# Sums of a 2x2 product scheme chained in PSUM, and scores issued behind a share of feed-forward

## The chip, the cores and the metric

The kernel runs on one core of a Trainium2 chip. The metric is the device time of one execution in microseconds (us). A core has five engines with instruction streams of their own: PE (TensorE, matrix products and transposes), ACT (ScalarE), DVE (VectorE), POOL (GpSimd) and SP (SyncE, which here only issues DMAs). They work in order, each on its own stream, and wait for each other by semaphores. Here PE writes to PSUM, ACT reads it from there, and POOL works in SBUF.

## The reference

Top-32 attention over 8 batches and 8 heads (576 positions, head size 64), then a feed-forward layer with ELU, all in fp32:

```python
scores = scale * np.matmul(q, k.transpose(0, 1, 3, 2))      # 8 x 8 x 576 x 576
kth = np.partition(scores, -32, axis=-1)[..., -32:-31]
scores = np.where(scores >= kth, scores, -1e9)
attn = np.exp(scores - scores.max(-1, keepdims=True))
attn = attn / (attn.sum(-1, keepdims=True) + 1e-9)
x = np.matmul(attn, v).transpose(0, 2, 1, 3).reshape(4608, 512)
h = x @ w_in                                                # 512 x 2048
g = np.where(h > 0, h, np.exp(np.minimum(h, 0)) - 1)
out = g @ w_out                                             # 2048 x 512
```

## The kernel before

**Attention in steps.** The work is cut into 144 steps, each one pair of heads times one tile of 128 queries. A step goes through a pipeline that is spread over four turns of the main loop. In turn `n`:

- PE computes the scores of step `n + 2` (`scores`, L335: eight matmuls of 64x128 tiles into two score tiles of PSUM, `wide[0]` and `wide[1]`, both called `scps` in the profile), and ACT evicts them to SBUF, scaled (L343, one instruction for each head);
- DVE selects the 32nd largest of each row of step `n` (`select`): per head, four MAX8 (L355, L369) with three MATCH_REPLACE8 (L362) between. The turn's four passes are these four rounds;
- ACT masks and exponentiates step `n - 1` (`mask`, L396 and L397), with a difference that POOL forms (`spread`, L376), and POOL normalises it (`normalise`, L407 to L414);
- PE transposes the probabilities of step `n - 2` (`turn`, L433) in three parts: four blocks (main), one block (rest) and four blocks (other); ACT copies them out (L434). The rest block has no PSUM tile of its own: it is written to the end of `wide[1]`;
- when the steps that go together are turned, `attend` (L459) multiplies them with the values, in 128x64 tiles, and ACT copies the result into `xT`, the input of the feed-forward layer (L486).

The k and q halves of later batches are loaded by SP (L235) into a few buffers, transposed by DVE (L289) and kept in `kqT`; v is loaded by SP (L269, L276). In the first turns DVE, ACT and POOL also decode the weights `w_in` and `w_out` (L179 to L196), in pieces that hang on DVE's passes.

**Feed-forward in shares.** The 4608 tokens make blocks: six of one tile of 128 tokens and fifteen of two. A block's pieces join the list `ffn` when its `xT` is complete. `feed(n, 0.25)` is called four times in a turn and takes pieces from the list by a budget, which is worked out from what is due when. A block has 16 `hidden` pieces (L534; ACT applies the ELU's parts, L544 to L553; the last addition is on POOL, L504, or in the early part on DVE, L506). A one-tile block then has four `project` pieces (L562). A two-tile block has seven `product` pieces.

**The 2x2 scheme.** A two-tile block multiplies its activations (two row halves, two column halves of 1024: a11, a12, a21, a22) with `w_out` (b11, b12, b21, b22) by seven products in place of eight. `product(j)` first forms a sum of quarters on POOL (L580, 128x1024, in `combine`), runs eight matmuls of 256 columns (L624, which the profile shows as 16 records) into a PSUM tile, and has ACT copy the result out (L629). Four of the seven weights are differences of quarters (`differences`, L681), kept in DRAM; `stream` (L663) loads them on SP, 256 KB a tile, four tiles a product, six tiles ahead: each tile that a product has used makes SP ask for another. The partial results are put together by POOL in SBUF (L580 again, 128x256, seven sums a block), and `emit` (L585) sends the rows out on SP.

The order in which instructions are issued on each engine is that of the program text: the scheduler is switched to manual. Everything depends on it, since each engine and each DMA queue takes its work in that order.

Of the kernel before, what the change touches and what calls it, by code (L numbers as in the profile page):

```python
# [9 lines left out]
ALU = mybir.AluOpType  # L10
FP32 = mybir.dt.float32
# [69 lines left out]
def kernel(  # L81
# [9 lines left out]
    nc = tc.nc  # L91
    P = nc.NUM_PARTITIONS
    B, H, S, D = q.shape
    dm, dff = moe_w_in.shape[0], moe_w_in.shape[1] // 2
# [7 lines left out]
    NG = NF // 2  # L102
# [11 lines left out]
    def pool(name, bufs, **kw):  # L114
        return ctx.enter_context(tc.tile_pool(name=name, bufs=bufs, **kw))
# [12 lines left out]
    ps_f = pool("ps_f", 2, space=PSUM)  # L128
# [77 lines left out]
    def settle():  # L206

        if decode or late or blocks[0].left or any(x[3] == 0 for x in ffn):
            return
        raws.close()  # L210
        late["f"] = ctx.enter_context(tc.tile_pool(name="f", bufs=2))
        late["g"] = ctx.enter_context(tc.tile_pool(name="g", bufs=2))
        late["x"] = ctx.enter_context(tc.tile_pool(name="xt", bufs=2))
        late["e"] = ctx.enter_context(tc.tile_pool(name="e", bufs=2))
        late["t"] = ctx.enter_context(tc.tile_pool(name="t", bufs=TB))
        late["in"] = ctx.enter_context(tc.tile_pool(name="in", bufs=2))
# [109 lines left out]
    def scores(u):  # L326

        u.sc = scpool.tile([P, 2, S], FP32, tag="sc", name="sc")
        q0 = (QUERIES if u.t.b == 0 else S) + u.t.qt * P
        for half in range(2):  # L330
            for h, i, rows in u.heads:
                kq = kqT[u.t.b, h // 2]
                part = slice(i * D, (i + 1) * D)
                k0 = (KEYS if i == 0 and u.t.b == 0 else 0) + half * HS
                nc.tensor.matmul(  # L335
                    wide[i][rows, half, 0:HS],
                    kq[part, q0 : q0 + u.t.ql],
                    kq[part, k0 : k0 + HS],
                    start=True,
                    stop=True,  # L340
                )
        for i in range(2):
            nc.scalar.activation(  # L343
                u.sc[:, i, :].rearrange("p (a s) -> p a s", a=2),
                wide[i][:, :, 0:HS], AF.Copy, scale=scale,
            )
# [147 lines left out]
    def close_gates(keep=0, upto=None):  # L494

        while gates:
            put, group, dst, n, apart = gates[0]
            if put > place[0] - keep if upto is None else group > upto:  # L500
                return
            gates.pop(0)
            if apart:
                nc.gpsimd.tensor_tensor(dst, n, dst, ALU.add)  # L504
                continue
            nc.vector.scalar_tensor_tensor(  # L506
                out=dst, in0=n, scalar=-1.0, in1=dst, op0=ALU.add, op1=ALU.add
            )

    def ffn_pieces(blk):  # L510
# [65 lines left out]
        def quarter(s, h):  # L576
            return blk.gT[h][:, :, s * P : (s + 1) * P]

        def combine(dst, x, y, op):
            nc.gpsimd.tensor_tensor(dst, x, y, op)  # L580

        def emit(s):
            for t in blk.tiles[s]:
                p0 = t.cols.start - s * P
                nc.sync.dma_start(out[t.rows, :], blk.o[s][p0 : p0 + t.ql, :])  # L585

        def product(j):
            left, right = slice(0, W), slice(W, dm)
            while blk.after:
                blk.after.pop(0)()  # L590
            if j == 7:
                return
            if j == 0:
                close_gates(upto=(blk.number, NF - 1))
                blk.o = [opool.tile([P, dm], FP32, tag="osb", name="osb") for _ in range(2)]
                blk.e = [late["e"].tile([P, W], FP32, tag="e", name="e") for _ in range(2)]
            a11, a12 = quarter(0, 0), quarter(0, 1)
            a21, a22 = quarter(1, 0), quarter(1, 1)
            c11, c12 = blk.o[0][:, left], blk.o[0][:, right]
            c21, c22 = blk.o[1][:, left], blk.o[1][:, right]  # L600
            e0, e1 = blk.e[0][:], blk.e[1][:]
            x, name, dst, after = (
                (a11, "b11", c11, [(a21, a21, a22, ALU.add)]),
                (a12, "b21", c12, [(a11, a21, a11, ALU.subtract)]),
                (a21, "t1", c22, [(a12, a12, a11, ALU.subtract)]),
                (a22, "t4", e0, [(a21, a22, a11, ALU.subtract)]),
                (a11, "t2", c21, [(c21, c21, c11, ALU.add), (c11, c11, c12, ALU.add)]),
                (a12, "b22", c12, [(c12, c12, c21, ALU.add), (c12, c12, c22, ALU.add)]),
                (a21, "t3", e1, [
                    (c21, c21, e1, ALU.add), (c22, c22, c21, ALU.add),  # L610
                    (c21, c21, e0, ALU.add),
                ]),
            )[j]
            if j == 0:
                combine(*after.pop())
            sums = ps_f.tile([P, dm], FP32, tag="f", name="ops")[:, left]
            for f in range(NG):
                if name[0] == "b":
                    w = w_out[:, NG * (name[1] == "2") + f, right if name[2] == "2" else left]
                else:  # L620
                    if f % TF == 0:
                        t = streamed.pop(0)
                    w = t[:, f % TF, :]
                nc.tensor.matmul(sums, x[:, f, :], w, start=f == 0, stop=f == NG - 1)  # L624
                if name[0] == "t" and f % TF == TF - 1:
                    stream()
            if 0 < j < 4:
                combine(*after.pop())
            nc.scalar.copy(dst, sums)  # L629
            blk.after += [lambda x=x: combine(*x) for x in after]  # L630
            if j > 4:
                blk.after.append(lambda: emit(j - 5))

        part = HIDDEN[blk.slots]
        behind = 2 * NF if blk.number else 0
# [14 lines left out]
        ]  # L650

    streamed, ahead_of = [], [0]
    names = ("t1", "t4", "t2", "t3")

    def stream():

        k = ahead_of[0]
        ahead_of[0] += 1
        if k >= 4 * QT * sum(x.slots == 2 for x in blocks):
            return  # L660
        t = late["t"].tile([P, TF, W], FP32, tag="t", name="tw")
        src = kept[names[k // QT % 4], k % QT]
        nc.sync.dma_start(t[:], src[:].rearrange("p (f n) -> p f n", f=TF))  # L663
        streamed.append(t)
# [35 lines left out]
    while ends:  # L700
        n = 1 if len(blocks) <= J else 2
        blk = Block(len(blocks), len(ends[:n]))
# [4 lines left out]
    for b in range(B):  # L707
# [15 lines left out]
        for qts in orders[b]:  # L723
# [3 lines left out]
            for qt in qts:  # L727
                n = len(steps)
# [12 lines left out]
    for b in range(1, B):  # L741
        f = first[b]
# [17 lines left out]
    def feed(n, share):  # L760

        place[0] += 1
        close_gates(2 if n > tight + 3 else 6)
        fed["at"] = max(fed["at"], n)
        ahead = [(w - fed["sum"]) / (x - fed["at"]) for x, w in due if x > fed["at"]]
        if ahead:
            fed["over"] += max(0.0, share * min(ahead))
        fed["at"] += share
        while ffn and decoded[0] >= ffn[0][1] and 0.5 * ffn[0][0] <= fed["over"]:
            cost, _, piece, _ = ffn.pop(0)  # L770
            fed["over"] -= cost
            fed["sum"] += cost
            piece()
            settle()
# [22 lines left out]
    def step(n):  # L797
        return steps[n] if 0 <= n < NS else None
# [3 lines left out]
    for n in range(NS + 3):  # L802
        for fn, args in todo.pop(n, []):
            fn(*args)
        ahead, cur, prev, done = step(n + 2), step(n), step(n - 1), step(n - 2)
        passes = select(cur, n < tight) if cur else iter(range(4))
        if ahead and n > 1:
            scores(ahead)
        if prev and n > tight:
            spread(prev)  # L810
        next(passes)
        feed(n, 0.25)
        while closing:
            attend(closing.pop(0))
        if prev:
            mask(prev, 0, n <= tight)
        if n > 1:
            turn_qk()
        next(passes)
        feed(n, 0.25)  # L820
        if done:
            turn(done, main)
            turn(done, rest)
        if prev:
            mask(prev, 1, n <= tight)
        next(passes)
        feed(n, 0.25)
        if done:
            turn(done, other)
        next(passes)  # L830
        if prev:
            normalise(prev)
        feed(n, 0.25)
        turn_qk(True)
        if n < 2:
            scores(ahead)
# [36 lines left out]
```

## Time and profile before

| quantity | value |
|---|---|
| three runs | 1600.43, 1596.32, 1598.8 us (median 1598.8) |
| profiled execution | 1596.33 us, of which the span on the core is 1594.5 us |
| mean granted clock of PE | 0.983 |
| PE busy | 1525.4 us (96%) |
| DVE busy | 1450.7 us (91%) |
| ACT busy | 1196.4 us (75%) |
| POOL busy | 938.5 us (59%) |
| 128x1024 sums on POOL (L580) | 60 of 2.37 us |
| 128x256 sums on POOL (L580) | 75 + 30 of 0.73 us |
| copies of products on ACT (L629) | 75 + 30 of 0.37 us |

Busy shares are means over the whole span. PE's idle time lies nearly all in the first 416 us, where the weights are decoded and DVE's selection sets the pace; behind that both PE and DVE are close to always busy. PE's records are pipelined, so the end of one lies beyond the start of the next; the distance from start to start is what a record costs.

In the lines of waits that follow, the name behind the arrow is the instruction whose end released the waiting one; the figures are the time waited in all, the number of waits and the longest, or, in a group's line, the busy time and the mean. In the lines of the timeline the first two numbers are start and duration, `x` tells how many instructions are put together, and the bracket is the idle time before them with its releaser. A stretch's line gives its bounds and its length, the busy time of PE, weight loads, DVE, ACT and POOL with the number of instructions, the granted clock, the DMA share and GB/s.

### The profile page before, as it was taken

The page shows a single profiled execution, that of the slowest core. Times are in us where ns is not written, and L with a number is a line of the kernel's source. Part 1 is how long each engine was busy: PE and PEld are TensorE (multiplying, and loading weights), DVE is VectorE, ACT ScalarE, POOL GpSimd, SP SyncE. Part 2 cuts the span into 40 slices and gives each one's busy share as a digit, 9 for nine tenths or more (in the row PEclk, how much of TensorE's full clock was granted, in tenths as well). Part 3 has the DMA queues.
Part 4 walks back from the last instruction along what each step waited for, and adds up shares of the span by engine and source line. Part 5 has one row for each costly group of instructions (what it writes and reads, how often), then busy time and mean ns, then how long its engine had stood idle before and what let it go on. Part 6 is the DMA issues. An engine that isn't in the chain of part 4 may idle for free.

```text
span 1594.5 us, 28265 instructions
## 1 busy us (share of the span) xinstructions
PE 1525.4 (96%) x9492; PEld 1180.7 (74%) x9492; DVE 1450.7 (91%) x2976; ACT 1196.4 (75%) x2460; POOL 938.5 (59%) x1596
## 2 busy tenths in 40 slices
PE   4789989999899999999999999999999999999999
PEld 2476667667677778877787778877777777887886
DVE  6899999999999799999999789999999969999800
ACT  6897666779586868696878777777768786869652
POOL 4984546446556565656566656565655656666651
PEclk9889989999999999999999999999999999999999
DMA  8622233012402243214421343214240414030320
GB/s 243 196 80 38 61 75 115 7 23 43 122 31 89 62 102 78 80 41 110 93 83 45 83 97 84 67 49 100 42 139 1 134 17 133 9 119 1 119 62 25
DMA packets 224912, 123.47 MB, mean 77 GB/s; under 512 B 182272, under 2 KB 183296, under 8 KB 224768
## 3 DMA queue, kind: packets, MB, share of 16 engines
q1 hardware_dynamic: 223568, 121.38, 28.0%
q8 instruction: 75, 1.23, 0.3%
q14 instruction: 69, 0.57, 0.1%
q10 hardware_dynamic: 1200, 0.30, 0.1%
HBM read 108.00 MB, written 13.63 MB: 76 GB/s over the span
## 4 chain that ended last, share of the span: by engine, by line
PE 68%; DVE 17%; ACT 8%; issue 3%; POOL 3%; DMA 1%; SPq 0%; DVEq 0%; ACTq 0%; POOLq 0%
PE hps L534 24%; PE ops L624 22%; PE avps L459 8%; PE scps L335 8%; DVE wk L362 7%; PE eps L433 6%; DVE m L369 5%; DVE m L355 2%; ACT sc L397 1%; ACT sc L396 1%; POOL tw L681 1%; ACT et L434 1%; DVE raw L192 1%; ACT n L553 1%; ACT n L544 1%
## 5 line engine op out<-in xcount | busy, mean ns | idle before, releaser
L369 DVE MAX8 m<-wk 128x8 f32<-128x576 f32 x864 | 609.0, 746 | 0.7 <-POOL den L376 0.7
L534 PE MATMUL hps<-xT,w_in 128*128 128x256 f32 (+1 forms) x2688 | 560.0, 356 | 0.0
L534 PEld LDWEIGHTS hps<-xT,w_in 128*128 128x128 f32 x2688 | 441.8, 192 | 77.1 <-issue 34.9
L362 DVE MATCH_REPLACE8 wk<-m,wk 128x576 f32<-128x576 f32 x576 | 423.1, 742 | 0.0
L397 ACT ACTIVATE sc<-sc,den 128x576 f32<-128x576 f32 x288 | 223.5, 776 | 61.2 <-POOL den L376 46.5
L407 POOL TENSOR_SCALAR dene<-den 128x2 f32<-128x2 f32 x144 | 32.5, 226 | 398.4 <-ACT sc L397 395.7
L624 PE MATMUL ops<-tw,gT 128*128 128x256 f32 x960 | 224.1, 386 | 10.5 <-DMA tw<-kept 10.4
L396 ACT ACTIVATE sc<-sc,m 128x576 f32<-128x576 f32 x288 | 225.1, 782 | 8.2 <-DVE m L369 8.2
L335 PE MATMUL scps<-kqT 64*128 64x288 f32 (+1 forms) x1280 | 200.6, 446 | 32.0 <-ACT et L434 18.2
L414 POOL TENSOR_SCALAR sc<-sc,rec 128x576 f32<-128x576 f32 x288 | 214.4, 755 | 14.9
L504 POOL TENSOR_TENSOR gT<-n,gT 128x512 f32<-128x512 f32 x136 | 173.6, 1277 | 75.5 <-ACT n L553 75.4
L355 DVE MAX8 m<-sc 128x8 f32<-128x576 f32 x288 | 201.9, 742 | 15.2 <-ACT sc L343 11.8
L624 PEld LDWEIGHTS ops<-tw,gT 128*128 128x128 f32 x960 | 178.4, 191 | 47.5 <-DMA tw<-kept 12.0
L362 DVE MATCH_REPLACE8 wk<-m,sc 128x576 f32<-128x576 f32 x288 | 211.5, 742 | 0.0
L343 ACT ACTIVATE sc<-scps 128x576 f32<-128x576 f32 x288 | 171.4, 649 | 48.9 <-PE scps L335 48.9
L459 PE MATMUL avps<-et,vT 128*64 128x256 f32 (+2 forms) x2320 | 194.1, 310 | 9.5 <-ACT et L434 9.4
L459 PEld LDWEIGHTS avps<-et,vT 128*64 128x64 f32 x2320 | 130.2, 141 | 76.2 <-issue 33.6
L335 PEld LDWEIGHTS scps<-kqT 64*128 64x128 f32 (+1 forms) x1280 | 106.9, 183 | 98.1 <-issue 36.9
L433 PE MATMUL eps<-ident,sc 128*128 128x128 f32 x1152 | 174.6, 277 | 1.2 <-ACT xT L486 0.8
L434 ACT COPY et<-eps 128x512 f32<-128x512 f32 x288 | 164.6, 572 | 9.6 <-PE eps L433 7.3
L433 PEld LDWEIGHTS eps<-ident,sc 128*128 128x128 f32 x1152 | 142.0, 143 | 32.8 <-issue 9.6
L624 PE MATMUL ops<-w_out,gT 128*128 128x256 f32 x720 | 164.4, 381 | 0.1
(56 smaller groups left out, 1570.1 us busy)
## 6 DMA issues: line engine op xcount, KB each, us to landing
tw<-kept SPq DMA_DIRECT2D x240, 256.0 KB, 3.2
raw<-in_moe_w_in_dram SPq DMA_DIRECT2D x16, 512.0 KB, 4.9
vT<-in_v_dram SPq DMA_DIRECT2D x64, 128.0 KB, 2.6
raw<-in_moe_w_out_dram SPq DMA_DIRECT2D x16, 512.0 KB, 4.2
out_dram<-osb SPq DMA_DIRECT2D x32, 256.0 KB, 2.4
kin<-in_k_dram SPq DMA_DIRECT2D x112, 72.0 KB, 2.4
qin<-in_q_dram SPq DMA_DIRECT2D x112, 72.0 KB, 2.5
kept<-tw SPq DMA_DIRECT2D x16, 256.0 KB, 2.0
```

Of the source, the lines that this page charges most:

```text
L335: nc.tensor.matmul(wide[i][rows, half, 0:HS], kq[part, q0 : q0 + u.t.ql], kq[part, k0 : k0 + HS], start=True, stop=True,)
L355: nc.vector.max(found[i], cur[i])
L362: nc.vector.match_replace(wk[i], found[i], cur[i], TAKEN)
L369: nc.vector.max(found[i], cur[i])
L396: nc.scalar.activation(sc, sc, AF.Prelu, scale=-1.0, bias=low, alpha=1.0 / STEEP)
L397: nc.scalar.activation(sc, sc, AF.Exp, scale=-STEEP, bias=gap, accum_out=u.den[:, i : i + 1])
L414: nc.gpsimd.tensor_scalar(u.sc[:, i, :], u.sc[:, i, :], rec[:, i : i + 1], 1.0, ALU.mult, ALU.mult)
L433: nc.tensor.transpose(ps[:, c * P : (c + 1) * P], sc[:, c0 : c0 + P], ident[:])
L434: nc.scalar.copy(g.et[:, chunks, u.at, :], ps[:, 0 : n * P].rearrange("p (c q) -> p c q", c=n),)
L459: nc.tensor.matmul(ps[i * D : (i + 1) * D, cols], vt[:, 2 * J + i if c == J else i * J + c, :], w, start=(c == 0), stop=(c == J),)
L534: nc.tensor.matmul(blk.h[:, f % bank, :], w_in[:, i, f * P : (f + 1) * P], blk.xT[:, i, 0:n_tok], start=(i == 0), stop=(i == NC - 1),)
L624: nc.tensor.matmul(sums, x[:, f, :], w, start=f == 0, stop=f == NG - 1)
```

## The change

There are two parts.

First, a block holds two PSUM tiles for all of its seven products, and three of their halves collect sums: `one` takes b11, then t2, then t3 on top of each other, `three` takes t1 and then b22, and `two` takes b21 and, opened anew, t4. ACT copies a half out after each product, the running sum included. The order of the products changes from b11, b21, t1, t4, t2, b22, t3 to b11, b21, t1, t2, b22, t3, t4, and with it the order in which the weights are streamed. POOL's sums of results go from seven to four a block; the four sums of quarters stay, in another order, and the a21 - a22 - a11 one is read by the last product. The first tile's rows are sent out one product earlier.

Second, from turn 2 on `scores(n + 2)` is issued behind the first share of feed-forward of its turn, directly ahead of `attend`, in place of the turn's start. On PE and on ACT (whose evictions are issued with it) the share and its activations now come first.

```diff
+                blk.s = [ps_f.tile([P, dm], FP32, tag="f", name="ops") for _ in range(2)]
...
-            x, name, dst, after = (
-                (a11, "b11", c11, [(a21, a21, a22, ALU.add)]),
-                (a12, "b21", c12, [(a11, a21, a11, ALU.subtract)]),
-                (a21, "t1", c22, [(a12, a12, a11, ALU.subtract)]),
-                (a22, "t4", e0, [(a21, a22, a11, ALU.subtract)]),
-                (a11, "t2", c21, [(c21, c21, c11, ALU.add), (c11, c11, c12, ALU.add)]),
-                (a12, "b22", c12, [(c12, c12, c21, ALU.add), (c12, c12, c22, ALU.add)]),
-                (a21, "t3", e1, [
-                    (c21, c21, e1, ALU.add), (c22, c22, c21, ALU.add),
-                    (c21, c21, e0, ALU.add),
+            one, two, three = blk.s[0][:, left], blk.s[1][:, left], blk.s[1][:, right]
+            x, name, sums, opens, dst, after = (
+                (a11, "b11", one, True, c11, [(a21, a21, a22, ALU.add)]),
+                (a12, "b21", two, True, e0, [(a11, a21, a11, ALU.subtract)]),
+                (a21, "t1", three, True, c22, [
+                    (a12, a12, a11, ALU.subtract), (c11, c11, e0, ALU.add),
                 ]),
+                (a11, "t2", one, False, c12, [(a21, a22, a11, ALU.subtract)]),
+                (a12, "b22", three, False, e1, [(c12, c12, e1, ALU.add)]),
+                (a21, "t3", one, False, c21, [(c22, c22, c21, ALU.add)]),
+                (a22, "t4", two, True, e0, [(c21, c21, e0, ALU.add)]),
             )[j]
             if j == 0:
-                combine(*after.pop())
-            sums = ps_f.tile([P, dm], FP32, tag="f", name="ops")[:, left]
+                combine(*after.pop(0))
...
-                nc.tensor.matmul(sums, x[:, f, :], w, start=f == 0, stop=f == NG - 1)
+                nc.tensor.matmul(
+                    sums, x[:, f, :], w, start=opens and f == 0, stop=f == NG - 1,
+                    skip_group_check=not opens,
+                )
...
             if 0 < j < 4:
-                combine(*after.pop())
+                combine(*after.pop(0))
             nc.scalar.copy(dst, sums)
             blk.after += [lambda x=x: combine(*x) for x in after]
-            if j > 4:
-                blk.after.append(lambda: emit(j - 5))
+            if j in (4, 6):
+                blk.after.append(lambda: emit(j // 2 - 2))
...
-    names = ("t1", "t4", "t2", "t3")
+    names = ("t1", "t2", "t3", "t4")
...
         passes = select(cur, n < tight) if cur else iter(range(4))
-        if ahead and n > 1:
-            scores(ahead)
         if prev and n > tight:
             spread(prev)
         next(passes)
         feed(n, 0.25)
+        if ahead and n > 1:
+            scores(ahead)
         while closing:
             attend(closing.pop(0))
```

## The prediction

> **What bounds the kernel now.** I read the engine totals first, then the busy time by stage, then PE's waits, then the order of records around the edit.
>
> ```profile
> PE 1525.4 (96%) x9492; PEld 1180.7 (74%) x9492; DVE 1450.7 (91%) x2976; ACT 1196.4 (75%) x2460; POOL 938.5 (59%) x1596
> ```
> ```profile
> 280.00:416.00 136.00, 130.38 (x744) 91.88 (x743) 134.79 (x279) 106.08 (x215) 69.14 (x131) 0.99 0.14 28
> 416.00:800.00 384.00, 380.68 (x2348) 300.26 (x2348) 372.79 (x767) 298.24 (x615) 229.15 (x404) 1.00 0.31 81
> 800.00:1200.00 400.00, 395.17 (x2458) 313.48 (x2456) 386.32 (x796) 310.91 (x641) 245.47 (x421) 1.00 0.29 79
> 1200.00:1520.00 320.00, 318.03 (x1986) 252.85 (x1986) 294.21 (x608) 248.34 (x515) 197.39 (x333) 1.00 0.23 67
> ```
>
> The second view is busy time by stretch: length, then PE, weight loads, DVE, ACT, POOL, clock, DMA. To 416 us DVE has no idle time and PE waits. Behind it PE does (1094 of 1104 us), so only what changes PE's stream there counts. POOL has 40% to spare: the 45 sums it loses (30 x 0.73 us of 128x256 with `osb` alone and 15 with `e`, 33 us in all) are worth nothing by themselves.
>
> ```profile
> PE scps L335 <- ACT et L434: 18.2, 9, 3.3
> PE ops L624 <- DMA tw<-kept: 10.4, 3, 5.6
> PE avps L459 <- ACT et L434: 9.4, 14, 1.0
> ```
>
> These are PE's waits: us, times, longest. The first lies before 280 us, where PE has slack. The second is three stalls, at 410 (5.62), 744 (1.38) and 1155 us (3.44), each in a streamed product whose weights were asked for late.
>
> **The change, part by part.**
>
> *Fewer shape switches on PE.* Scores are 64x128 tiles, value products 128x64, all else 128x128. Record to record a 256-column matmul takes 215 ns; the first of another shape takes 309 and the one behind it 105 ns too much, so a switch costs 0.2 us. With the scores directly ahead of the value products the built program has 391 switches for 445. Of the 54, 17 come before the stall at 410 us and are swallowed by it; 10 lie between 410 and 744 us (-2.0 us), 16 to 1155 (-3.2), 11 behind (-2.2). Bounds: 0.1 to 0.25 us each.
>
> *The rest transpose meets the eviction.* The rest transpose (L433, one 128x128) writes the unused end of a score bank, so it waits until ACT has evicted these scores (L343).
>
> ```profile
> 518.49 0.27 ACT L434 COPY et<-scps 128x128 f32<-128x128 f32 x1
> 520.28 0.59 ACT L434 COPY et<-eps 128x512 f32<-128x512 f32 x1
> 521.45 1.19 ACT L343 ACTIVATE sc<-scps 128x576 f32<-128x576 f32 x2 [0.58 <-PE scps L335]
> ```
>
> Here ACT stood ready and the two evictions ended 1.29 us behind the last score record (520.17 + 1.17, to 522.64). Before, a feed share (a product or hidden piece) lay between scores and transposes, so nothing waited. In the new order 11 steps behind 410 us run scores, four main transposes (0.44 us), rest transpose: no value product comes due in them and the share now stands ahead. The gap is 1.29 - 0.44 = 0.85 us: 3 steps to 744 us (+2.6), 3 to 1155 (+2.6), 5 behind (+4.3). In 17 more, one hidden piece lies between, 2.27 us; there ACT may first have to finish activations of the share ahead (four of 0.59 to 0.63 us, ending some 2.2 to 2.45 us behind), so 0 to 0.3 us, taken as 0.15 (+0.9, +0.9, +0.8). Where a value product is between (1.8 to 2.3 us and more) it covers. What queues behind the waiting transpose is all of PE, since matmuls run in order. Bounds 0 and 1.2 us a step.
>
> *The stream of weights.* It is asked for on SP in order, a tile for each tile used, six ahead. The last two tiles of a block (3 and 4 of the last product) are asked for by the last streamed product but one. That was followed by one more streamed product and one resident one; now the final product comes straight behind it, and the resident `b22` is past. So the request is one product (3.55 us) later against its use, and falls behind k and q loads (L235) that wait for a DVE transpose (L289) in two blocks. In block 8 (all four rows are of the kernel before):
>
> ```profile
> 1080.30 3.62 PE L624 MATMUL ops<-w_out,gT 128*128 128x256 f32 x16
> 1087.33 3.72 PE L624 MATMUL ops<-tw,gT 128*128 128x256 f32 x16
> ```
> ```profile
> 1089.54 0.76 DVE L289 STREAM_TRANSPOSE kqT<-kin 128x576 f32<-128x576 f32 x1
> ```
> ```profile
> 1090.32 0.33 SPq L235 DMA_DIRECT2D kin<-in_k_dram  x1
> ```
>
> At 1080.30 stands the last product but one (after: `t3`), at 1087.33 the last (after: `t4`), whose third tile begins 1.8 us in, at 1089.1. SP is held to 1090.3, issues two k loads (0.96) and then the tile; tiles land 3.2 us behind their issue (the page's median for `tw`). 1094.5 - 1089.1 = 5.4 us of stall. A stall of 5.62 us at 410 was followed by a half clock (8 records in 3.77 us for 1.89, +1.9 us), one of 3.44 by none; I add 1.9: +7.3 in all. In block 4 the same reckoning (transpose 759.33, last product 760.55): landing 764.5, wanted 762.3, +2.3 us and no half clock. In the other blocks no such load stands ahead, or the transpose it needs is long done. Bounds: 0 (tiles just in time) to 4 in block 4, 0 to 9 in block 8. The Trainium skill, "TensorE: Matmul & The Clock Gate", What's actually happening, has PE drop to half rate after one idle window of about 3.4 us that runs free of the kernel; by it a stall of 5.4 us may miss a whole window, and the sum would be 1.9 us lower; the trace's two long stalls, one with and one without, fit.
>
> *The old stalls.* At 410: with scores behind the first share ACT does two weight-decoding steps earlier near 46 us, where DVE waited 3.92 us for it, and one k load less stands ahead of the stream: PE resumes 1.8 us earlier (between 0 and 4). At 744: the landing follows DVE, which waits for the scores at 550 us ("DVE kqT L289 <- PE scps L335", three times, 37.8 us), now 1.7 us later; no gain. At 1155: DVE last followed PE at 921 us, so the landing moves with PE as of then (+2 to 3), while PE will be 7 or more later still by block 8: the 3.44 us are gone (-3.4).
>
> *The chains.* Sums are read three to five products in as before, with one POOL sum of 0.73 us ahead of `c22`'s operand; slack was 1.4 us and more save in one block: +0 to 1. The second and third product share a PSUM tile, so the third waits for ACT's copy (0.37 us, some 0.36 behind the product); in 4 of 15 blocks only 0.44 us of transposes stand between: 4 x 0.3 = 1.2 at most. Together +1, between 0 and 3; at nothing only if ACT is idle just then. The Trainium skill, "PSUM — Partial Sum Buffer", Summary: rules for kernel authors, wants PSUM guarded by bank when one engine reads what another fills; by that rule these waits can't be had away while the two halves share a bank. No run here shows it otherwise.
>
> **The sum**, against the profiled execution (1596.3 us, span 1594.5; the median of the three runs, 1598.8, is 2.5 higher):
>
> - to 744 us: -1.8 - 2.0 + 2.6 + 0.9 = -0.3; the kept wait at 744 puts it at about +0.8;
> - to 1155 us: block 4 +2.3, -3.2 + 2.6 + 0.9 = +0.3, block 8 +7.3, the old stall -3.4: +6.5;
> - behind: -2.2 + 4.3 + 0.8 = +2.9; chains +1.
>
> Together +11.2 us: 1607.5 for the execution; against the median 1610. Since block 8's price is the most uncertain I shade it by two and say 1608.
>
> **The rivals.**
>
> *Faster: the switches alone.* If ACT gets to the evictions in time or the tile framework lets the rest transpose go, the 28 waits are nothing, and if SP isn't held (DVE running some 5 us further ahead of PE than before, the point from which it decides), the stream is in time. Then -1.8 - 7.4 + 1 = -8 us, 1590. For it: DVE had waits for PE of up to 13.7 us, so it is ahead in places. Against: the rows in block 8 place the transpose behind the product already, with nothing in the change that hastens DVE there. Chance 0.24.
>
> *The evictions bite, the stream does not.* 0.8 + 0.3 + 2.9 + 1, that is +5: 1604. For it: stalls on the stream were three in 1596 us, and DMA latency varies. Chance 0.18.
>
> *Both bite*, as forecast: 1601 to 1616. Chance 0.5.
>
> *Worse:* the 17 short covers fail by a full 0.85 us (+12) or the half clock follows in block 4 too: 1617 to 1625. For it: ACT is 75% busy, and the evictions stand behind its activations now. Chance 0.08.
>
> *It does not do what it says* is no rival for the switches and the sums: both counts are in the built program.
>
> **How the numbers follow.** About 0.3% (4.8 us) is what a measurement of this kernel can tell from no change: 1594.0 to 1603.6. Faster takes the first rival's 0.24 less 0.02 for its slower end; same takes that 0.02, half of the second rival's chance less a little (0.08) and 0.06 of the forecast's low end: 0.16. The rest, 0.62, is slower. The range runs from 1591, which takes in the upper part of the first rival, to 1617, where only the worse case is beyond. The forecast's own range is 1601 to 1616.
>
> **What would show it.** Right: a new PE wait "scps L433 <- ACT sc L343" of 10 us or so in 11 to 28 places; a stall on `tw` near 1090 us of 3 us or more, one near 762, none near 1155; POOL busy 33 us less; gaps ahead of L335 and L459 fewer. Wrong: no wait at the rest transposes, or `tw` waits that sum to no more than 10.4 us, in which case it is the first rival.

## The result, and the profile after

The changed kernel takes 1605.4 us (median of six runs, 1604.2 to 1609.4) against 1598.5 of the kernel before: 1.0048 times as long, 95% interval 1.0031 to 1.0064, so 5 to 10 us slower. The forecast was 1608 us with 0.62 for slower. The profiled execution has a span of 1603.8 us, 9.3 more than before.

Two things in the description above have to be corrected. The manual order holds for PE, ACT, DVE and POOL alone; SP's order is laid out by the scheduler, which matters below. And the sum of quarters that is formed last (a22 - a11 in the code's names) is read by t3, not by the last product.

The totals by engine, then busy time by stretch (bounds, length, PE, weight loads, DVE, ACT, POOL, clock, DMA share, GB/s), of the changed kernel:

```profile
PE 1523.6 (95%) x9492; PEld 1182.3 (74%) x9492; DVE 1452.6 (91%) x2976; ACT 1200.0 (75%) x2460; POOL 903.3 (56%) x1551
```
```profile
416.00:800.00 384.00, 376.24 (x2331) 297.19 (x2329) 372.47 (x768) 298.33 (x614) 216.86 (x388) 1.00 0.30 79
800.00:1200.00 400.00, 391.18 (x2430) 310.52 (x2429) 383.20 (x788) 307.49 (x631) 232.20 (x403) 0.99 0.30 79
1200.00:1520.00 320.00, 313.74 (x1954) 248.78 (x1954) 294.80 (x608) 245.62 (x507) 185.41 (x318) 1.00 0.23 67
```

POOL is 35 us less busy and nothing came of it (its 45 sums fewer are 60 fewer with `osb` alone and 15 more with `e`). PE is busy for 1.8 us less in all, yet the kernel is longer: PE waits more behind 416 us, 22.8 us of 1104 instead of 10.1. PE's waits, in us, times and the longest:

```profile
PE scps L433 <- ACT sc L343: 12.2, 17, 0.8
PE ops L624 <- DMA tw<-kept: 11.9, 5, 5.0
PE scps L335 <- ACT et L434: 11.4, 6, 2.6
PE avps L459 <- ACT et L434: 9.8, 16, 1.9
```

The first row did not exist before: the rest transpose that waits for the eviction of the scores. One of the 17, in the timeline of PE and then of ACT (start, duration):

```profile
1146.13 1.24 PE L335 MATMUL scps<-kqT 64*128 64x288 f32 x8
1147.30 0.66 PE L433 MATMUL eps<-ident,sc 128*128 128x128 f32 x4
1148.73 0.30 PE L433 MATMUL scps<-ident,sc 128*128 128x128 f32 x1 [0.78 <-ACT sc L343]
```
```profile
1147.40 1.19 ACT L343 ACTIVATE sc<-scps 128x576 f32<-128x576 f32 x2 [0.79 <-PE scps L335]
```

ACT stood ready, started at once and ended at 1148.59; PE had only four transposes in between. From start to start PE loses 0.94 us here, as in ten other steps behind 410 us. Of the six others five lie earlier; the last, at 1386 us, is shorter (0.51 us), with a short value product in between.

The second row has a sum 1.5 us above that of before (10.4) and other places. The new long stall is in block 8 (PE, then SP):

```profile
1087.03 1.99 PE L624 MATMUL ops<-tw,gT 128*128 128x256 f32 x8
1094.06 3.78 PE L624 MATMUL ops<-tw,gT 128*128 128x256 f32 x8 [5.04 <-DMA tw<-kept]
```
```profile
1090.25 0.87 SPq L235 DMA_DIRECT2D kin<-in_k_dram  x2
1091.22 1.39 SPq L666 DMA_DIRECT2D tw<-kept  x3
```

The first half of the last product is through at 1089, the tiles of the second half are asked for at 1091.22, behind two k loads that waited for DVE. Behind the stall eight records take 3.78 us for 1.99: half the clock. The next is in block 4:

```profile
760.77 3.27 PE L624 MATMUL ops<-tw,gT 128*128 128x256 f32 x8 [2.39 <-DMA tw<-kept]
```

A third is short, and its cause another: SP was held not by a k load but by the first tile's output rows, which waited for a sum on POOL until 590.92 (PE, then SP). The same hold returns at the end of the experiments.

```profile
594.66 1.13 PE L624 MATMUL ops<-tw,gT 128*128 128x256 f32 x4 [0.96 <-DMA tw<-kept]
```
```profile
590.95 0.36 SPq L585 DMA_DIRECT2D out_dram<-osb  x1
591.40 1.36 SPq L666 DMA_DIRECT2D tw<-kept  x3
```

The steps' rest transposes, set against those of the kernel before, give the course: 1.3 us earlier at 408 us, 5.8 at 424, 3.5 at 742, 0.1 later at 764, 0.3 earlier at 1080, 7.2 later at 1091, 8.2 at 1152, 4.4 at 1165 and 9.2 at the end. So the loss has four main places: the two long new stalls (4.3 and 7.5 us with their half clocks), and two slopes of 2.2 us (424 to 742, of which the short new stall is 1.2) and 4.8 us (behind 1165); 1.0 us more comes between 1091 and 1152. Two old stalls gave back 4.5 and 3.7 us, the one at 744 another 0.6.

### The profile page after: what moved, and what is told of

The parts are those of the page before. It is cut to its first block, busy times and chain, and to the rows that moved or that the text cites. A ratio compares the mean times of both kernels' runs of the same rounds, so it can differ in the third digit from the quotient of the medians.

```text
span 1603.8 us, 28233 instructions
## 1 busy us (share of the span) xinstructions
PE 1523.6 (95%) x9492; PEld 1182.3 (74%) x9492; DVE 1452.6 (91%) x2976; ACT 1200.0 (75%) x2460; POOL 903.3 (56%) x1551
## 4 chain that ended last, share of the span: by engine, by line
PE 67%; DVE 13%; ACT 11%; POOL 5%; issue 3%; DMA 1%; SPq 0%; DVEq 0%; ACTq 0%; POOLq 0%
PE hps L534 24%; PE ops L624 18%; PE avps L459 8%; PE scps L335 7%; DVE wk L362 6%; PE eps L433 5%; DVE m L369 4%; PE ops L562 2%; ACT sc L397 2%; ACT sc L343 2%; DVE m L355 2%; ACT sc L396 1%; POOL tw L684 1%; ACT et L434 1%; POOL sc L414 1%
## 5 line engine op out<-in xcount | busy, mean ns | idle before, releaser
L534 PE MATMUL hps<-xT,w_in 128*128 128x256 f32 (+1 forms) x2688 | 550.8, 354 | 3.5 <-ACT gT L547 3.5
L624 PE MATMUL ops<-tw,gT 128*128 128x256 f32 x960 | 224.5, 387 | 12.8 <-DMA tw<-kept 11.9
L335 PE MATMUL scps<-kqT 64*128 64x288 f32 (+1 forms) x1280 | 196.6, 447 | 25.5 <-ACT kqT L311 13.4
L624 PEld LDWEIGHTS ops<-tw,gT 128*128 128x128 f32 x960 | 178.9, 192 | 46.0 <-DMA tw<-kept 14.5
L624 PE MATMUL ops<-w_out,gT 128*128 128x256 f32 x720 | 164.3, 381 | 0.1
```

The lines of the kernel that those rows point to most:

```text
L335: nc.tensor.matmul(wide[i][rows, half, 0:HS], kq[part, q0 : q0 + u.t.ql], kq[part, k0 : k0 + HS], start=True, stop=True,)
L534: nc.tensor.matmul(blk.h[:, f % bank, :], w_in[:, i, f * P : (f + 1) * P], blk.xT[:, i, 0:n_tok], start=(i == 0), stop=(i == NC - 1),)
L624: nc.tensor.matmul(sums, x[:, f, :], w, start=opens and f == 0, stop=f == NG - 1, skip_group_check=not opens,)
```

## The experiments

My theory was that of the prediction: a gain by fewer shape switches, a loss by the evictions and one by weights that are asked for too late. All times are medians; the kernel before, run beside them, had 1598.4 to 1598.8.

**One part at a time.** First the scores moved alone:

```diff
-        if ahead and n > 1:
-            scores(ahead)
...
         feed(n, 0.25)
+        if ahead and n > 1:
+            scores(ahead)
```

> The scores moved, the products as before. My theory (the loss is rest transposes that wait for the score evictions, plus a weight stream that asks too late; the switches are a gain): rest transposes wait about 0.94 us in 11 steps behind 410 us (+10.3), 37 fewer switches there at 0.2 us (-7.4), the start some 4 to 6 us earlier, and the stalls on the weights at 744 and 1155 us stay, none new near 758 and 1089. Sum -3 to +2 us on the kernel before: 1596 to 1600 us, clearly under the changed kernel's 1605.4. Rival one (later scores starve DVE's selection, so that the moved scores are the whole loss): 1603 to 1606, with DVE waiting for L343 in many steps. Rival two (the chained sums are the whole loss, the move is a pure gain): 1588 to 1592.

Measured: 1598.0 us, ratio 1.000 (0.9991 to 1.0008). The rest transposes wait 12.1 us in 17 places, as in the changed kernel; no stall at 758 or 1089, and those at 740 (2.0 us from start to start) and 1151 (3.1) stay. Neither rival holds: the move is neither the loss nor a gain. It starts 5.3 us early at 424 us and loses 4.9 to the end.

Then the chained sums and the new order of products alone:

```diff
         passes = select(cur, n < tight) if cur else iter(range(4))
+        if ahead and n > 1:
+            scores(ahead)
...
         feed(n, 0.25)
-        if ahead and n > 1:
-            scores(ahead)
```

(against the changed kernel, whose other lines it keeps)

> The sums chained in PSUM and the product order new, the scores where they were. My theory: no wait at the rest transposes and 445 shape switches as before, but the new stalls on the weights: about 2.4 us near 758 us with a half clock behind it (+1.4) and 5 us near 1089 us with a half clock (+2), while the 3.4 us at 1155 go; +1 for chains. Sum +6 to +9 us on the kernel before: 1604 to 1608. Rival one (the moved scores are the whole loss; 45 sums fewer on POOL help): 1595 to 1599. Rival two (sharing banks makes each product wait for the copy of the one before): 1609 or more, with PE waits for ACT's copies at L624.

Measured: 1603.7 us, ratio 1.0035 (1.0023 to 1.0048), just under the forecast's 1604. This part alone carries most of the loss, 5.2 of 7.0 us; the scores alone gained 0.4, so some 2 us belong to neither part by itself. PE's view of block 8:

```profile
1089.34 1.99 PE L624 MATMUL ops<-tw,gT 128*128 128x256 f32 x8
1096.64 1.65 PE L624 MATMUL ops<-tw,gT 128*128 128x256 f32 x3 [5.31 <-DMA tw<-kept]
```

The stall near 758 us is not there; the one at 744 is 0.4 us longer instead and has a half clock behind it. The step from 1080 to 1091 us is 7.7 us longer than before, and the stall at 1155 is gone (-3.7). No wait for a product's copy shows at L624, so the rival of the shared banks falls.

**The order of the products.** The changed kernel with t3 ahead of b22:

```diff
-                    (a12, a12, a11, ALU.subtract), (c11, c11, e0, ALU.add),
+                    (a21, a22, a11, ALU.subtract), (c11, c11, e0, ALU.add),
                 ]),
-                (a11, "t2", one, False, c12, [(a21, a22, a11, ALU.subtract)]),
-                (a12, "b22", three, False, e1, [(c12, c12, e1, ALU.add)]),
+                (a11, "t2", one, False, c12, [(a12, a12, a11, ALU.subtract)]),
                 (a21, "t3", one, False, c21, [(c22, c22, c21, ALU.add)]),
+                (a12, "b22", three, False, e1, [(c12, c12, e1, ALU.add)]),
...
-            if j in (4, 6):
-                blk.after.append(lambda: emit(j // 2 - 2))
+            if j > 4:
+                blk.after.append(lambda: emit(j - 5))
```

> The changed kernel with one edit: t3 is multiplied ahead of b22, so that the last two weight tiles of a block are asked for one product earlier against their use, as in the kernel before (the sum of quarters that t3 reads is formed one product earlier too). My theory: the stalls near 758 us (2.4 and 1.4 of half clock) and 1089 us (5 and 2) go, the one at 1155 us comes back (3.4 to 3.8): -7 to -8 us, 1597 to 1599. Rival (DMA latency, not the place in the queue, makes the stalls): they stay, 1604 to 1606. Risk: t3's sum of quarters has only one product of cover, so a POOL wait at L624 of up to 1 us a block (+0 to +15).

Measured: 1601.3 us, ratio 1.0020 (1.0011 to 1.0029): 4 us less, not 7 to 8. Both long new stalls are gone, the short one too, and that at 1155 is back (3.25 us), as expected, so the place in the queue makes them. Behind the stall at 1155 stands a half clock that the scores-only kernel has not (1.4 us). The rest went the way of the risk: from 1165 us to the end this kernel falls 5.7 us back where the scores-only one falls 3.0, with small waits of PE at the products, the longest for a sum of quarters on POOL (0.51 us) and for ACT's copy of a product (0.46).

**The wait at the rest transposes.** If this transpose is simply put later, its wait should go:

```diff
         if done:
             turn(done, main)
-            turn(done, rest)
...
         if done:
+            turn(done, rest)
             turn(done, other)
```

> The changed kernel with one edit: the rest transpose (into the end of a score bank) is issued behind the third share, ahead of the other transposes, instead of straight behind the main ones. My theory: 8 of the 11 waits of 0.94 us behind 410 us go (in 3 steps nothing lies between even now), so -7 to -8 us: 1597 to 1599, with 'scps L433 <- ACT sc L343' down from 12.2 us to 2 to 4. The stalls on the weights stay. Rival (the waits are only where PE's idle time shows and would turn up elsewhere, since ACT is the late one): 1603 to 1606, the wait moving to another line.

Measured: 1613.2 us, ratio 1.0095 (1.0077 to 1.0113). The expectation was wrong, and the rival right in its direction, though not in its size. The old wait fell to 2.3 us, as I had said, and another grew from 11.4 us:

```profile
PE scps L335 <- ACT et L434: 44.2, 23, 5.4
PE scps L433 <- ACT sc L343: 2.3, 3, 0.8
```

The shared bank binds in both directions: the next turn's scores overwrite the rest block, so they wait until ACT has copied it out, and ACT gets to that behind a mask and a share's activations (PE, then ACT):

```profile
1138.72 0.27 PE L433 MATMUL scps<-ident,sc 128*128 128x128 f32 x1
1143.08 1.23 PE L335 MATMUL scps<-kqT 64*128 64x288 f32 x6 [1.25 <-ACT et L434]
```
```profile
1142.78 0.25 ACT L434 COPY et<-scps 128x128 f32<-128x128 f32 x1
```

The other way to take the wait away is to move the scores only in turns in which value products are due; in the others the move saves no switch.

```diff
+        if ahead and n > 1 and not closing:
+            scores(ahead)
...
         feed(n, 0.25)
+        if ahead and n > 1 and closing:
+            scores(ahead)
         while closing:
```

It was applied to the kernel before, to the changed kernel, and to the one with t3 ahead of b22.

> The kernel before, with the scores moved only in turns in which value products are due; in the other turns they stay at the turn's start. The built program has the same 391 shape switches as the kernel with all scores moved, but a share of feed-forward lies between scores and rest transpose wherever no value product does. My theory: the 11 waits of 0.94 us of the scores-only run go and nothing else changes: 1598.0 - 10 = 1587 to 1589, 'scps L433 <- ACT sc L343' near 1 or 2 us. Rival (PE's time behind 410 us is set by DVE or ACT, so a wait taken away comes back as another): 1595 to 1599.

> The changed kernel with the same edit: scores moved only where value products are due. My theory: 1605.4 - 10 = 1594 to 1597, with the stalls on the weights near 758 and 1089 us left as they are. Rival as for the kernel with products as before: 1602 to 1606.

> Both edits on the changed kernel: t3 ahead of b22, scores moved only where value products are due. My theory: 1601.3 - 10 = 1590 to 1593, some 3 us above the one with the products as before, because the chained sums have less cover on POOL (three waits of 0.3 to 0.7 us for L580) and give nothing on PE. Rival (45 sums fewer on POOL are worth something once PE has no other waits): at or under the one with the products as before.

Measured: 1596.3 (ratio 0.9987, 0.9978 to 0.9996), 1600.2 (1.0009, 1.0000 to 1.0018) and 1599.1 us (1.0004, 0.9995 to 1.0013). All three are above what my theory gave, and the first lies where its rival had it. The waits at the rest transposes are all but gone, but only 2 to 5 us came of the 10. PE's waits in the first of the three tell where they went:

```profile
PE ops L624 <- DMA tw<-kept: 15.1, 3, 5.6
```

The three old stalls end when the weights land that SP asks for behind k loads, and these wait for DVE's transposes. The one ahead of the second stall, in the kernel before and in the first of the three:

```profile
738.73 0.75 DVE L289 STREAM_TRANSPOSE kqT<-kin 128x576 f32<-128x576 f32 x1
```
```profile
736.11 0.76 DVE L289 STREAM_TRANSPOSE kqT<-kin 128x576 f32<-128x576 f32 x1
```

The transposes come 4.0, 2.6 and 2.0 us earlier than in the kernel before and the stalls end 4.3, 2.6 and 1.1 us earlier, but PE is 4.2, 5.2 and 3.3 us ahead when it gets there. So the first stall keeps its length and PE waits longer in the others: 5.7, 4.2 and 5.7 us from start to start, with half clocks behind all three, for 5.8, 1.5 and 3.6 before, with one behind the first alone. On my theory the stalls had to stay as they were; I had treated them as fixed durations, where DVE sets their ends.

**The stalls themselves.** With a ring of seven tiles (`TF, TB = 2, 7`) on the first of these kernels:

> As the kernel before with scores moved where value products are due, and the ring of streamed weight tiles seven long for six. My theory of the stalls (a request held on SP behind k and q loads, a tile worth 0.89 us of products): each of the three stalls (about 3, 2 and 3 us) shrinks by 0.9 us, together with what half clock follows -2 to -4 us on the one with six: 1584 to 1586. Rival (the landing is set by DVE's transpose alone, and the held tile is the same one however long the ring): no change.

Measured: 1594.4 us, ratio 0.9968 (0.9955 to 0.9980): 1.9 us less than with six, just short of the 2 to 4 that were forecast, with PE's waits for `tw` down from 15.1 to 11.9 us. The 1584 to 1586 us were missed, since the kernel with six tiles had not come down to the time from which they were reckoned.

Then SP's instructions in the order of the text, so that the k and q loads no longer stand ahead of weight requests:

```diff
-    engines = {E.PE, E.Activation, E.DVE, E.Pool}
+    engines = {E.PE, E.Activation, E.DVE, E.Pool, E.SP}
```

on the kernel with scores moved where values are due, on the changed kernel, on the kernel before, and on the changed kernel with scores moved where values are due.

> The kernel with products as before and scores moved where value products are due, and one more edit: SP's instructions too go in the order of the program text, where the scheduler had laid them out. By that order no k or q load that waits for DVE's transposes stands ahead of a weight request that PE needs sooner. My theory (PE's gain was given back in three stalls on the weights, 5.7, 4.2 and 5.7 us, and in the half clock behind them, some 2 us each): they go, 1596.3 - 18 to 21 = 1575 to 1579. Rival (DVE sets the time up to 1155 us and the stalls are where PE's lead over it shows): 1592 to 1597, with PE waiting elsewhere for DVE's work, or DVE waiting for loads that come later now.

> The changed kernel with SP's instructions in the order of the text. My theory: its stalls on the weights (3.1, 0.8, 2.6, 5.2 us) and some 4 us of half clock go: 1605.4 - 14 to 16 = 1589 to 1592; the waits of 0.94 us at the rest transposes stay. Rival (latency of the DMAs or a DVE that sets the time): 1600 to 1605.

> The kernel before with SP's instructions in the order of the text: its stalls (5.8, 1.5, 3.6 us, with 1.9 us of half clock behind the first) go: 1598.4 - 10 to 13 = 1585 to 1588. The one with scores moved where value products are due should then be lower by the switches alone, 37 x 0.2 = 7 us or so, and the start's 2 to 4. Rival as for that one: 1594 to 1599.

> The changed kernel with scores moved only where value products are due and SP in the order of the text, so that the chained sums are the only difference from the kernel with products as before. My theory: the chained sums cost PE 2 to 4 us in waits for POOL's sums of quarters and give it nothing: 1578 to 1583. Rival (with PE's other waits gone, 45 sums fewer on POOL pay): the same as that one or 1 to 3 us less.

| kernel, SP in the order of the text | us | ratio to the kernel before |
|---|---|---|
| products as before, scores where values are due | 1574.3 | 0.9847 (0.9834 to 0.9860) |
| the changed kernel | 1626.5 | 1.0175 (1.0161 to 1.0189) |
| the kernel before | 1582.6 | 0.9898 (0.9885 to 0.9912) |
| the changed kernel, scores where values are due | 1616.3 | 1.0108 (1.0094 to 1.0121) |

The first and the third came out as forecast or a little better: no wait of PE for `tw` is left in them, and the gain of the moved scores shows at last, 8.4 us between the two. Stretches of the first:

```profile
416.00:800.00 384.00, 381.06 (x2404) 304.10 (x2403) 382.31 (x788) 305.56 (x631) 236.81 (x418) 1.00 0.29 75
1200.00:1520.00 320.00, 318.39 (x1998) 256.46 (x1998) 278.68 (x575) 244.72 (x509) 200.63 (x334) 1.00 0.26 71
```

DVE is now 382 of 384 us busy in the first of them: little is left to gain there on PE alone.

With the chained sums the same edit does the opposite of what I expected:

```profile
PE ops L624 <- DMA tw<-kept: 27.6, 15, 6.4
```

(the fourth kernel). Fifteen stalls, one or so in each block. SP, PE and POOL near one of them:

```profile
588.62 0.34 SPq L585 DMA_DIRECT2D out_dram<-osb  x1
589.05 1.83 SPq L666 DMA_DIRECT2D tw<-kept  x4
```
```profile
588.54 1.99 PE L624 MATMUL ops<-tw,gT 128*128 128x256 f32 x8
591.79 2.02 PE L624 MATMUL ops<-tw,gT 128*128 128x256 f32 x8 [1.25 <-DMA tw<-kept]
```
```profile
586.42 1.48 POOL L414 TENSOR_SCALAR sc<-sc,rec 128x576 f32<-128x576 f32 x2
587.86 0.73 POOL L580 TENSOR_TENSOR osb<-osb,e 128x256 f32<-128x256 f32 x1
```

In text order the first tile's rows are sent out just ahead of t3, before SP may ask for the tiles that t3 sets free; they need a sum that POOL makes behind its normalising, at 588.59. So the last two weight tiles are late in nearly every block. It is the same weakness by another path, and that of the short stall at 594 us in the changed kernel: in the new order only one and a quarter products lie between request and use, and whatever SP waits for ahead of them stalls PE. With the products as before one more lies between.

## Why the prediction was right

*Direction and mechanism.* All three steps that decided were there: the waits at the rest transposes, the stalls in blocks 4 and 8, the lost stall at 1155. The rival of a gain by switches alone fails on both of its conditions in the trace above; the rival in which the stream does not bite fails by block 8. Of the worse case one condition came true, the half clock in block 4, without its time, since the start gave more than forecast.

*Fewer switches* (0.2 us each, 37 behind 410). Where nothing gives the time back, between the kernels with SP in text order, PE gains 5.1 us from 424 us to the last steps, although its waits at the value products grow by about 0.5 us in five places and one of 0.7 us from start to start is new: 5.1 + 2.5 + 0.7 = 8.3 us, 0.22 each. Confirmed.

*The rest transposes.* 11 waits behind 410 us, as counted, of 0.94 for 0.85 us, and a twelfth of 0.5 behind a value product that was held to cover. The 17 short covers, taken at 0.15 us, waited nothing: 2.6 us too much in the sum.

*The stream.* Block 8 was forecast at 7.3 and took 7.5. Block 4 was forecast at 2.3 and took 4.3: the stall was sized rightly (2.39), but I had given it no half clock because it was shorter than the 3.44 us one that had none. That step failed. And the short stall at 594 us (1.2 us of time) was not foreseen: in the other blocks I had looked for k and q loads ahead of the tiles, and not for the output rows.

*The old stalls.* At 1155 forecast 3.4 off, measured 3.7. At 410 PE was to resume 1.8 us earlier; it resumed 4.0 us earlier (411.7 for 415.7), at the bound, and the half clock of the kernel before (412.5 to 419.3 us) did not come: 5.8 us earlier at 424, the largest miss. It belongs to the moved scores: the scores-only kernel is 5.3 us early there, the chain-only one 0.3. DVE's wait for ACT's decoding fell as I said (5.1 to 2.6 us before 90 us, 3.1 with the scores alone). But I had also said that DVE has no idle time to 416 us, and that was wrong: from 90 to 280 us it was busy for 187.2 of 190 us, waiting for POOL, and in both kernels with moved scores for 190.0. That these 2.8 us brought PE forward is argued, not shown by itself. The wait at 744, which was to be kept, shrank by 0.8 us.

*The chains*, +1: set against the scores-only kernel, four steps behind 1165 us take 0.3 to 0.8 us more, 1.8 us in all; the kernel with t3 ahead of b22 pays more (2.7).

The sum was +11.2 for the execution, and its span grew by 9.3. By stretch:

| stretch | forecast | measured |
|---|---|---|
| to 753 us, with the stalls at 410 and 744 | +0.8 | -4.2 |
| block 4 | +2.3 | +4.3 |
| the rest to 1152 us | +0.3 | +0.6 |
| block 8 | +7.3 | +7.5 |
| the stall at 1155 | -3.4 | -3.7 |
| behind it, with the chains | +3.9 | +4.8 |

So 5 us too little credit at the start stood against 3 us too little debt behind it. The mechanisms were right; that the total came so close is in part luck. The median grew by 7.0 us.

## What to carry to other kernels

A stall whose end is set by another engine is not a fixed duration: what one engine saves ahead of it, beyond what the other one saves too, is given back in it, and an edit is best judged with such stalls out of the way (here the scores moved where values are due were worth 2 us, or 8, by the same edit). When an order of work is changed, ask for every buffer and every queued transfer how much lies between request and use afterwards, and what the queue's own engine waits for ahead of it. A PSUM bank lent to a second purpose binds both ways: moving one user away from a wait can move it nearer to the other.

## What the runs showed of the hardware

The half clock does not go by the length of a stall alone. In the changed kernel it followed one of 2.39 us (block 4); in the kernel before one of 3.44 us at 1155 was followed by none. Two stalls of the same 1.81 us differ too: the first row is of the chain-only kernel, with a half clock behind it, the second of the scores-only kernel, with none; the third is the one of 3.44 us.

```profile
746.00 2.95 PE L624 MATMUL ops<-tw,gT 128*128 128x256 f32 x8 [1.81 <-DMA tw<-kept]
```
```profile
742.05 1.99 PE L624 MATMUL ops<-tw,gT 128*128 128x256 f32 x8 [1.81 <-DMA tw<-kept]
```
```profile
1158.04 2.01 PE L624 MATMUL ops<-tw,gT 128*128 128x256 f32 x8 [3.44 <-DMA tw<-kept]
```

PE's granted clock around the stall of block 4, in stretches (bounds, length, PE busy, clock, DMA share, GB/s):

```profile
757.00:761.00 4.00, 1.61 (x8) 1.00 0.74 185
761.00:765.00 4.00, 4.00 (x14) 0.57 1.01 287
765.00:769.00 4.00, 4.00 (x22) 1.00 1.05 302
```

The Trainium skill, "TensorE: Matmul & The Clock Gate", What's actually happening, gives an idle window of about 3.4 us that runs free of the kernel. The traces bear out that the length alone does not decide; they differ in that 2.39 us of idle time, and once 1.81, were enough. What else decides is open.
